# Float64 weights made float32: loaded two bytes further on, and put together from integer parts

## The chip, the cores and the metric

The kernel runs on one core of one Trainium2 chip, as a single launch. The metric is the device time of that launch in microseconds. Three runs of the kernel before gave 390.85, 390.97 and 391.49 us; the median is 390.97 us.

A core has five engines that run side by side, each through its own list of instructions, in order: TensorE (PE in the profile, with its weight loads as PEld), VectorE (DVE), ScalarE (ACT), GpSimd (POOL) and SyncE (SP), which here does nothing but issue transfers. Sixteen DMA engines carry the transfers.

## The reference, cut to what matters

A Mamba-2 scan over `x`, `a`, `B`, `C` (4 sequences, 8 heads, 768 steps) gives 3072 tokens of 256 numbers. They pass through a normalised SwiGLU network:

```
rms = np.sqrt(np.mean(x * x, axis=-1, keepdims=True) + 1e-06)
xn = x / rms * rms_g
g = xn @ w_gate                       # 256 x 1536
silu = g * (1.0 / (1.0 + np.exp(-g)))
val = xn @ w_val                      # 256 x 1536
return (silu * val @ w_out).astype(np.float32)   # 1536 x 256
```

The three weight matrices are drawn as float32 and then multiplied by a float64 scalar, so they arrive as float64: 8 bytes a number, 3 x 1536 x 256 of them. [...] A float64 is one sign bit, 11 bits of exponent and 52 of mantissa; seen as four 16-bit words in memory, word 3 (the last) holds the sign, the exponent and the first 4 bits of the mantissa, and words 0, 1 and 2 hold the rest from the bottom up.

## The kernel before, in words

All work is written as a flat list of small steps. Two dictionaries (`first_kinds`, `kinds`) name them, and a long string `order` gives their sequence by hand: `0:man.3` is the step `man` with argument 3 of block 0. Every engine gets its instructions in the sequence of that string; nothing is re-ordered later. Six blocks of 512 tokens follow one another; the scan of a block is done beside the network of the block before it. The network of blocks 1 to 5 uses fast matrix products of the Strassen kind (`product_gv`, L965, and `product_o`, L1086), on sums of weights that are made once (`combine_w`, L934). Block 0 uses plain products (L879, L889, L997) in its first part, while the weights still come in.

The weights come in 18 pieces of 512 numbers on each of 128 partitions (512 KB each): pieces 0 and 1 hold 128 columns of both gate and value matrix, pieces 2 to 11 hold 256 columns of one of the two, pieces 12 to 17 hold two row blocks of the output matrix. Each piece takes four named steps:

- `fetch.k` (L171) issues the transfers from SP into a buffer `wr`, of which there are six in turn. Pieces 0 and 1 take two transfers of 256 KB with rows of 1024 bytes, all others one of 512 KB with rows of 2048 bytes.
- `pow.k` (`power`, L217) makes the power of two and the sign, as bfloat16, with three ScalarE activations (all on line L215): word 3 to an int16, that to float32, that to the int16 whose bits are the bfloat16.
- `man.k` (`mantissa`, L231) makes the mantissa as a float32 between 2^20 and 2^21 in magnitude, with two VectorE instructions: L234 (masks of the high 32-bit word, with the leading one set) and L237 (adds the low word times 2^-32).
- `wt.k` (`weight`, L240) multiplies the two into `wgv` or `wo`, with one VectorE instruction, L243.

A buffer `wr` is free for the next piece after the first ScalarE step, L234 and L237 have read it. The tile `e` of the power shares its four buffers with the copies `p` that the fast products need (L971).

Pieces 0 to 9 and 11 are converted before the steps of the fast products begin in `order` (with `P.2.3`); piece 10 and the six pieces of the output matrix are converted between those products.

Of the kernel before, what the change touches and what calls it, by code (L numbers as in the profile page):

```python
# [9 lines left out]
FP32 = mybir.dt.float32  # L10
I32 = mybir.dt.int32
I16 = mybir.dt.int16
U32 = mybir.dt.uint32
BF16 = mybir.dt.bfloat16
AF = mybir.ActivationFunctionType
ALU = mybir.AluOpType
# [4 lines left out]
def kernel(  # L21
# [33 lines left out]
    nc = tc.nc  # L55

    P = 128
# [5 lines left out]
    DM, DF = moe_w_gate.shape  # L63
# [10 lines left out]
    const = ctx.enter_context(tc.tile_pool(name="const", bufs=1))  # L74
    raw = ctx.enter_context(tc.tile_pool(name="raw", bufs=3))
    ssd = ctx.enter_context(tc.tile_pool(name="ssd", bufs=2))
    cvt = ctx.enter_context(tc.tile_pool(name="cvt", bufs=2))
# [77 lines left out]
    wo = const.tile([P, NF, DM], FP32, name="wo")  # L155

    def words(w):
        t = w.tensor
        return dataclasses.replace(
            t, dtype=I32, shape=tuple(t.shape[:-1]) + (2 * t.shape[-1],)).ap()  # L160

    wsrc = {"g": words(moe_w_gate).rearrange("(t p) f -> p t f", p=P),
            "v": words(moe_w_val).rearrange("(t p) f -> p t f", p=P),
            "o": words(moe_w_out).rearrange("(o i) m -> i o m", i=P)}
    wdst = {"g": wg, "v": wv, "o": wo}
    pieces = [("gv", 0, P), ("gv", P, P)]
    pieces += [(n, c, 256) for c in range(256, DF, 256) for n in "gv"]
    pieces += [("o", c, 2) for c in range(0, NF, 2)]
    fetched = {}

    def fetch(*ks):  # L171
        for k in ks:
            n, c, w = pieces[k]
            if n == "o":
                src, dst, shape = wsrc[n][:, c:c + w], wo[:, c:c + w], (w, DM)
            else:
                src, shape = [wsrc[m][:, :, 2 * c:2 * (c + w)] for m in n], (2 * len(n), w)
                dst = (wgv.rearrange("p n k f -> p (n k) f") if n == "gv" else
                       wdst[n])[:, :, c:c + w]
            r = raw.tile([P, shape[0], 2 * shape[1]], I32, tag="wr", name="wr", bufs=6)  # L180
            if n == "o":
                nc.sync.dma_start(out=r, in_=src)
            else:
                for m, of in enumerate(src):
                    nc.sync.dma_start(out=r[:, 2 * m:2 * m + 2], in_=of)
            w32 = r.rearrange("p k (f w) -> p k f w", w=2)
            w16 = r.bitcast(I16).rearrange("p k (f w) -> p k f w", w=4)
            fetched[k] = (w16[:, :, :, 3], (w32[:, :, :, 0], w32[:, :, :, 1]), dst,
                          [P] + list(shape))

    parts = {}
# [3 lines left out]
    def functions(name):  # L202

        if loaded[0] != name:
            loaded[0] = name
            if name == "silu":
                nc.scalar.preload_act_table(AF.Silu)
            else:
                nc.scalar.preload_act_table_set("natural_log_exp_and_others")

    def activation(**operands):
        kind = {AF.Silu: "silu", AF.Exp: "exp", AF.Ln: "exp"}.get(operands["func"])
        if kind:
            functions(kind)
        nc.scalar.activation(**operands)  # L215

    def power(k):  # L217
        words16, (lo, hi), dst, shape = fetched[k]
        n = shape[1] * shape[2]
        e = cvt.tile([P, n], FP32, tag="e", name="e", bufs=4)  # L220
        k16 = e.bitcast(I16)[:, n:2 * n].rearrange("p (a b) -> p a b", a=shape[1])
        g = e.rearrange("p (a b) -> p a b", a=shape[1])
        b16 = e.bitcast(I16)[:, 0:n].rearrange("p (a b) -> p a b", a=shape[1])
        activation(out=k16, in_=words16, func=AF.Relu, scale=1.0 / 16, bias=kinks[:, 0:1])
        activation(out=g, in_=k16, func=AF.Prelu, scale=-1.0, bias=kinks[:, 1:2],
                             alpha=2.0 ** -20)
        activation(out=b16, in_=g, func=AF.Prelu, scale=-2.0 ** 27, bias=kinks[:, 2:3],
                             alpha=2.0 ** -20)
        parts[k, "e"] = b16.bitcast(BF16)

    def mantissa(k):  # L231
        words16, (lo, hi), dst, shape = fetched[k]
        m = cvt.tile(shape, I32, tag="m", name="m")
        nc.vector.tensor_scalar(out=m, in0=hi, scalar1=0xFFFFF, scalar2=0x100000,  # L234
                                op0=ALU.bitwise_and, op1=ALU.bitwise_or)
        parts[k, "f"] = f = m.bitcast(FP32)
        nc.vector.scalar_tensor_tensor(out=f, in0=lo.bitcast(U32), scalar=2.0 ** -32, in1=m,  # L237
                                       op0=ALU.mult, op1=ALU.add)

    def weight(k):  # L240
        words16, (lo, hi), dst, shape = fetched[k]
        e, f = parts.pop((k, "e")), parts.pop((k, "f"))
        nc.vector.scalar_tensor_tensor(out=dst, in0=f, scalar=2.0 ** -20, in1=e,  # L243
                                       op0=ALU.mult, op1=ALU.mult)

    a_sb = ffn.tile([NAR, 2 * P], FP32, tag="ob", name="a_sb", bufs=1)
    warm = const.tile([P, 256], BF16, name="warm")
# [15 lines left out]
    ident16 = const.tile([P, P], BF16, name="ident16")  # L263
    whole16 = const.tile([P, P], BF16, name="whole16")
    never16 = const.tile([P, HC], BF16, name="never16")
    kinks = const.tile([P, 3], FP32, name="kinks")
    mean = const.tile([P, P], FP32, name="mean")
    eps = const.tile([P, 1], FP32, name="eps")
    tmask = const.tile([P, 2], FP32, name="tmask")
# [63 lines left out]
            nc.vector.tensor_copy(out=never16[r], in_=never[r, r])  # L333

    def kinks_of_powers():
        for k, v in enumerate((1152.0 - 7.5 / 16, 256.0, -1792.0 * 128.0)):
            nc.vector.memset(kinks[:, k:k + 1], v)

    def idle(n):
# [23 lines left out]
    def minus_mid():  # L363
# [17 lines left out]
                                               op0=ALU.mult),  # L381
        "mid": from_middle, "middles": from_middles,
        "never16": mask16, "ident16": lambda: nc.vector.tensor_copy(out=ident16, in_=ident),
        "whole16": lambda: nc.vector.tensor_copy(out=whole16, in_=never),
        "kinks": kinks_of_powers, "eps": lambda: nc.vector.memset(eps, 1e-6),
        "mean": lambda: nc.vector.memset(mean, 1.0 / DM),
        "tmask": lambda: nc.vector.reduce_sum(
            out=tmask, in_=hmask.rearrange("p (q t) -> p t q", t=2), axis=AX.X),
# [9 lines left out]
    rows, ps = {}, {}  # L398
# [797 lines left out]
    def by_vector(out, in_, scale):  # L1196
# [22 lines left out]
        "yt": lambda p: taken_out(p, ac.copy),  # L1219
        "ydone": lambda p: leave(("y", p)),  # L1220
        "pow": power, "man": mantissa, "wt": weight,
        "ms": norm_sums, "rs": norm_roots, "rb": spread_roots, "xn": norm_apply,
        "early": lambda f, s: products_early(
# [15 lines left out]
        "cw": combine_w, "cwp": lambda j, k: combine_w(j, k, nc.gpsimd), "o": first_projection,  # L1239
        "tx": combine_x, "txp": lambda blk, k: combine_x(blk, k, nc.gpsimd),  # L1240
        "fetch": fetch, "put": put,
    }

# [249 lines left out]
```

## Time and profile before

| | |
|---|---|
| median of three runs | 390.97 us (390.85 to 391.49) |
| span of the profiled execution, first to last instruction | 389.5 us |
| PE busy | 383.3 us (98%) |
| DVE busy | 289.8 us (74%) |
| ACT busy | 226.4 us (58%) |
| POOL busy | 152.0 us (39%) |
| granted TensorE clock | 1.000 |
| DMA packets, bytes | 109940, 28.05 MB |

The profile shows one execution. Its span runs from the first to the last instruction; 390.97 - 389.5 = 1.5 us of the median run lie around it, and the page gives no other time for the profiled execution. "Busy" is the union of the times of an engine's instructions. For PE it is a weak sign, since matmuls overlap and their ends are modelled: an idle time of PE is real, but a busy one can hide waiting, which shows as a group of matmuls that takes longer than the same group elsewhere. A transfer's "landing" is the time from its issue until its semaphore tells that the data is there.

### The profile page before, as it was taken

How to read it: one execution, taken by the hardware profiler on the slowest of the kernel's cores; microseconds unless marked ns; L12 is line 12 of the kernel's file. 1: busy time of each engine (PE TensorE's matmuls, PEld its weight loads, DVE VectorE, ACT ScalarE, POOL GpSimd, SP SyncE). 2: the span in 40 equal slices, each digit the busy share in tenths (PEclk: the TensorE clock that was granted, in tenths of full speed). 3: DMA queues.
4: the chain of work that ended last, by engine and by line, in shares of the span. 5: the costliest groups of instructions: out<-in, count | busy, mean ns of one | idle time of the engine just before them, and what ended most of it. 6: DMA issues, size and time to landing. Idle time of an engine off the chain costs nothing.

```text
span 389.5 us, 9637 instructions
## 1 busy us (share of the span) xinstructions
PE 383.3 (98%) x3805; PEld 329.8 (85%) x3805; DVE 289.8 (74%) x612; ACT 226.4 (58%) x471; POOL 152.0 (39%) x168
## 2 busy tenths in 40 slices
PE   8999999999999999999999999999999999999996
PEld 5676478788888999888899988899888899988995
DVE  6999999997976988669594765768374577454684
ACT  2899979988767262665865234763444571345420
POOL 5022045523693455343577701364611234212231
PEclk9999999999999999999999999999999999999999
DMA  8978984474073414634336112000100001000001
GB/s 107 241 153 259 240 195 147 120 157 42 3 101 86 50 13 94 145 42 96 70 78 81 27 42 42 2 15 22 56 3 2 2 12 50 29 0 0 2 0 56
DMA packets 109940, 28.05 MB, mean 72 GB/s; under 512 B 94824, under 2 KB 103752, under 8 KB 109896
## 3 DMA queue, kind: packets, MB, share of 16 engines
q1 hardware_dynamic: 107816, 27.31, 32.8%
q8 instruction: 30, 0.49, 0.5%
q10 hardware_dynamic: 2080, 0.13, 0.4%
q14 instruction: 14, 0.11, 0.1%
HBM read 23.69 MB, written 3.74 MB: 70 GB/s over the span
## 4 chain that ended last, share of the span: by engine, by line
PE 87%; DVE 9%; issue 2%; ACT 1%; DVEq 0%; ACTq 0%
PE gate L965 29%; PE o L1086 23%; PE val L965 21%; PE o L997 5%; PE y L750 3%; PE g L613 1%; DVE wgv L243 1%; DVE m L237 1%; DVE m L234 1%; DVE hid L912 1%; PE g L606 1%; PE e L474 1%; PE y L678 1%; DVE L L652 1%; ACT yt L821 0%
## 5 line engine op out<-in xcount | busy, mean ns | idle before, releaser
L977 DVE TENSOR_TENSOR c<-val,p 128x512 f32<-128x512 f32 x99 | 67.4, 686 | 45.1 <-PE val L965 33.3
L971 ACT COPY p<-gate 128x512 f32<-128x512 f32 x99 | 56.8, 581 | 57.5 <-PE gate L965 55.4
L965 PE MATMUL gate<-tx,wgv 128*128 128x256 f32 x264 | 65.9, 381 | 0.0
L215 ACT ACTIVATE c<-c 128x256 f32<-128x256 f32 x99 | 40.0, 415 | 38.7 <-DVE c L977 38.4
L990 POOL TENSOR_TENSOR hid<-c 128x256 f32<-128x256 f32 x31 | 24.7, 800 | 87.1 <-ACT c L215 83.1
L965 PEld LDWEIGHTS gate<-tx,wgv 128*128 128x128 f32 x264 | 49.2, 190 | 7.3 <-ACT p L971 0.7
L1117 DVE TENSOR_TENSOR ob<-ob,o 128x128 f32<-128x128 f32 (+1 forms) x90 | 24.2, 298 | 21.7 <-PE o L1086 16.9
L990 DVE TENSOR_TENSOR hid<-c 128x256 f32<-128x256 f32 x68 | 34.5, 521 | 6.9 <-ACT c L215 6.7
L1086 PE MATMUL o<-two,hid 128*128 128x128 f32 x280 | 36.5, 276 | 0.1
L1086 PEld LDWEIGHTS o<-two,hid 128*128 128x128 f32 x280 | 34.5, 192 | 1.1 <-DVE hid L990 0.4
L965 PE MATMUL val<-xn,wgv 128*128 128x256 f32 x132 | 33.7, 381 | 0.0
L965 PE MATMUL val<-tx,sw 128*128 128x256 f32 x132 | 33.5, 380 | 0.0
L965 PE MATMUL val<-xn,sw 128*128 128x256 f32 x132 | 33.3, 381 | 0.0
L965 PE MATMUL gate<-tx,sw 128*128 128x256 f32 x132 | 33.1, 381 | 0.0
L965 PE MATMUL gate<-xn,wgv 128*128 128x256 f32 x132 | 32.8, 381 | 0.0
L507 POOL TENSOR_SCALAR_AFFINE_SELECT L<-L 64x512 f32<-64x512 f32 x32 | 23.6, 737 | 18.6 <-ACT L L215 17.4
L965 PEld LDWEIGHTS val<-xn,wgv 128*128 128x128 f32 x132 | 24.8, 190 | 3.5
L965 PEld LDWEIGHTS val<-tx,sw 128*128 128x128 f32 x132 | 24.8, 190 | 3.5 <-issue 0.2
L965 PEld LDWEIGHTS gate<-tx,sw 128*128 128x128 f32 x132 | 24.7, 190 | 3.5 <-ACT p L971 0.2
L965 PEld LDWEIGHTS gate<-xn,wgv 128*128 128x128 f32 x132 | 24.3, 190 | 3.4 <-DVE hid L912 0.3
L965 PEld LDWEIGHTS val<-xn,sw 128*128 128x128 f32 x132 | 24.4, 190 | 3.2 <-issue 0.2
L215 ACT ACTIVATE e<-e,kinks 128x512 f32<-128x512 int16 (+1 forms) x36 | 26.0, 722 | 1.2
(203 smaller groups left out, 717.0 us busy)
## 6 DMA issues: line engine op xcount, KB each, us to landing
L<-rowd SPq DMA_DIRECT2D x32, 128.0 KB, 3.4
xr<-in_x_dram SPq DMA_DIRECT2D x24, 128.0 KB, 3.2
wr<-in_moe_w_out_dram SPq DMA_DIRECT2D x6, 512.0 KB, 5.6
out_dram<-ob SPq DMA_DIRECT2D x24, 128.0 KB, 1.8
wr<-in_moe_w_gate_dram SPq DMA_DIRECT2D x5, 512.0 KB, 5.8
wr<-in_moe_w_val_dram SPq DMA_DIRECT2D x5, 512.0 KB
br<-in_B_dram SPq DMA_DIRECT2D x23, 64.0 KB, 2.6
dT<-rowe SPq DMA_DIRECT2D x10, 128.0 KB
```

What stands on the lines that cost most here:

```text
L215: nc.scalar.activation(**operands)
L234: nc.vector.tensor_scalar(out=m, in0=hi, scalar1=0xFFFFF, scalar2=0x100000, op0=ALU.bitwise_and, op1=ALU.bitwise_or)
L237: nc.vector.scalar_tensor_tensor(out=f, in0=lo.bitcast(U32), scalar=2.0 ** -32, in1=m, op0=ALU.mult, op1=ALU.add)
L507: nc.gpsimd.affine_select(out=L[r], in_=L[r], pattern=[[0, L.shape[1]], [1, HC]], compare_op=ALU.is_ge, fill=0.0, base=0, channel_multipli ...
L750: nc.tensor.matmul(out=y[2 * k + u][rows, (2 * n + i) * HC:(2 * n + i + 1) * HC], start=(k, u, rows.start) not in opened, stop=True, skip_ ...
L965: nc.tensor.matmul(out=dst[:, half[w]], lhsT=lhsT, rhs=rhs, start=(k in (1, 2, 5) and w == 0), stop=True, skip_group_check=True)
L971: nc.scalar.copy(out=t, in_=Xs[j])
L977: nc.vector.tensor_tensor(out=t, in0=Zs[j], in1=a, op=ALU.add)
L990: engine.tensor_tensor(out=hid[:, 2 * j + c // 10 - 1, c % 10 - 1], in0=u, in1=src[:, half[1]], op=ALU.mult)
L997: nc.tensor.matmul(out=o, lhsT=hid[:, f, k // 2, (k % 2) * P:(k % 2 + 1) * P], rhs=wo[:, f], start=opens, stop=(f == NF - 1), skip_group_c ...
L1086: nc.tensor.matmul(out=Os[blk, b][:, place * P:(place + 1) * P], lhsT=hidden_or_sum(u)[:, g], rhs=rhs, start=(blk, b) not in opened, stop= ...
L1117: nc.vector.tensor_tensor(out=o, in0=o, in1=src, op=ALU.add if what[0] == "+" else ALU.subtract)
```

## The change

Each row is fetched without its first two bytes. The transfer starts at the second 16-bit word of a row and takes one word less (2046 bytes of 2048, or 1022 of 1024), and lands at the start of the buffer's row. In the buffer every number's words are thereby shifted by one place: word 3 is found at place 2, and words 1 and 2, which were on either side of a 32-bit boundary, now are one aligned 32-bit word at place 0. Word 0, the lowest 16 bits, is not used any more.

- `power` has two ScalarE steps in place of three. The first turns word 3 into a float32, the second into an int32 that equals (word 3 - 14336) times 2^19 with the sign in the top bit: the float32's sign, exponent and first 4 mantissa bits.
- `mantissa` has one VectorE step in place of two: the 32-bit word times 2^-13, at most 2^19 - 1, as an integer. Those are the other 19 bits of the mantissa.
- `weight` puts the two together with a bitwise or of two int32 tiles (`tensor_tensor`), in place of the product of two tiles and a constant (`scalar_tensor_tensor`).
- `kinks`, the constants of the ScalarE steps, has two columns in place of three.

The string `order`, the pieces, the buffers and their number stay as they are. The lists of instructions of PE, POOL and SP keep their sequence and number; DVE's and ACT's lose the instructions named and keep the sequence of the others.

```diff
-            t, dtype=I32, shape=tuple(t.shape[:-1]) + (2 * t.shape[-1],)).ap()
+            t, dtype=I16, shape=tuple(t.shape[:-1]) + (4 * t.shape[-1],)).ap()
...
-                src, dst, shape = wsrc[n][:, c:c + w], wo[:, c:c + w], (w, DM)
+                src, dst, shape = [wsrc[n][:, c:c + w]], wo[:, c:c + w], (w, DM)
             else:
-                src, shape = [wsrc[m][:, :, 2 * c:2 * (c + w)] for m in n], (2 * len(n), w)
+                src, shape = [wsrc[m][:, :, 4 * c:4 * (c + w)] for m in n], (2 * len(n), w)
...
-            r = raw.tile([P, shape[0], 2 * shape[1]], I32, tag="wr", name="wr", bufs=6)
-            if n == "o":
-                nc.sync.dma_start(out=r, in_=src)
-            else:
-                for m, of in enumerate(src):
-                    nc.sync.dma_start(out=r[:, 2 * m:2 * m + 2], in_=of)
-            w32 = r.rearrange("p k (f w) -> p k f w", w=2)
-            w16 = r.bitcast(I16).rearrange("p k (f w) -> p k f w", w=4)
-            fetched[k] = (w16[:, :, :, 3], (w32[:, :, :, 0], w32[:, :, :, 1]), dst,
-                          [P] + list(shape))
+            r = raw.tile([P, shape[0], 4 * shape[1]], I16, tag="wr", name="wr", bufs=6)
+            for m, of in enumerate(src):
+                rows = of.shape[1]
+                nc.sync.dma_start(out=r[:, rows * m:rows * (m + 1), 0:4 * shape[1] - 1],
+                                  in_=of[:, :, 1:])
+            w16 = r.rearrange("p k (f w) -> p k f w", w=4)
+            w32 = r.bitcast(U32).rearrange("p k (f w) -> p k f w", w=2)
+            fetched[k] = w16[:, :, :, 2], w32[:, :, :, 0], dst, [P] + list(shape)
...
     def power(k):
-        words16, (lo, hi), dst, shape = fetched[k]
+        top, below, dst, shape = fetched[k]
         n = shape[1] * shape[2]
         e = cvt.tile([P, n], FP32, tag="e", name="e", bufs=4)
-        k16 = e.bitcast(I16)[:, n:2 * n].rearrange("p (a b) -> p a b", a=shape[1])
         g = e.rearrange("p (a b) -> p a b", a=shape[1])
-        b16 = e.bitcast(I16)[:, 0:n].rearrange("p (a b) -> p a b", a=shape[1])
-        activation(out=k16, in_=words16, func=AF.Relu, scale=1.0 / 16, bias=kinks[:, 0:1])
-        activation(out=g, in_=k16, func=AF.Prelu, scale=-1.0, bias=kinks[:, 1:2],
-                             alpha=2.0 ** -20)
-        activation(out=b16, in_=g, func=AF.Prelu, scale=-2.0 ** 27, bias=kinks[:, 2:3],
-                             alpha=2.0 ** -20)
-        parts[k, "e"] = b16.bitcast(BF16)
+        activation(out=g, in_=top, func=AF.Prelu, scale=-1.0, bias=kinks[:, 0:1],
+                   alpha=2.0 ** -40)
+        activation(out=g.bitcast(I32), in_=g, func=AF.Prelu, scale=-2.0 ** 59,
+                   bias=kinks[:, 1:2], alpha=2.0 ** -40)
+        parts[k, "e"] = g.bitcast(I32)
 
     def mantissa(k):
-        words16, (lo, hi), dst, shape = fetched[k]
-        m = cvt.tile(shape, I32, tag="m", name="m")
-        nc.vector.tensor_scalar(out=m, in0=hi, scalar1=0xFFFFF, scalar2=0x100000,
-                                op0=ALU.bitwise_and, op1=ALU.bitwise_or)
-        parts[k, "f"] = f = m.bitcast(FP32)
-        nc.vector.scalar_tensor_tensor(out=f, in0=lo.bitcast(U32), scalar=2.0 ** -32, in1=m,
-                                       op0=ALU.mult, op1=ALU.add)
+        top, below, dst, shape = fetched[k]
+        parts[k, "f"] = m = cvt.tile(shape, I32, tag="m", name="m")
+        nc.vector.tensor_scalar(out=m, in0=below, scalar1=2.0 ** -13, scalar2=2.0 ** 19 - 1,
+                                op0=ALU.mult, op1=ALU.min)
 
     def weight(k):
-        words16, (lo, hi), dst, shape = fetched[k]
+        top, below, dst, shape = fetched[k]
         e, f = parts.pop((k, "e")), parts.pop((k, "f"))
-        nc.vector.scalar_tensor_tensor(out=dst, in0=f, scalar=2.0 ** -20, in1=e,
-                                       op0=ALU.mult, op1=ALU.mult)
+        nc.vector.tensor_tensor(out=dst.bitcast(I32), in0=f, in1=e, op=ALU.bitwise_or)
...
-        for k, v in enumerate((1152.0 - 7.5 / 16, 256.0, -1792.0 * 128.0)):
+        for k, v in enumerate((-14336.0, -28672.0 * 2.0 ** 19)):
```

More of the change, by code (lines that the diff above doesn't have):

```diff
@@ L265 @@
     never16 = const.tile([P, HC], BF16, name="never16")
-    kinks = const.tile([P, 3], FP32, name="kinks")
+    kinks = const.tile([P, 2], FP32, name="kinks")
     mean = const.tile([P, P], FP32, name="mean")
```

## The prediction

> **What bounds the kernel now.** I began with the page's busy shares and its chain of waits (with the first and the last of the chain's pieces on DVE in this part: start, duration), then looked at the stretches in which weights are converted, and then at PE's own waits there.
>
> ```profile
> PE 383.3 (98%) x3805; PEld 329.8 (85%) x3805; DVE 289.8 (74%) x612; ACT 226.4 (58%) x471; POOL 152.0 (39%) x168
> PE 87%; DVE 9%; issue 2%; ACT 1%; DVEq 0%; ACTq 0%
> ...
> 16.18 0.06 DVE L L652
> ...
> 53.49 0.21 DVE A L692
> ```
>
> PE is idle for 389.5 - 383.3 = 6.2 us of the whole span, and the chain that ends last is PE for 87% of it. The 9% of DVE in that chain, about 35 us, lie together, from 16.2 to 53.7 us. The view by stretches shows that part (columns: PE, PEld, DVE, ACT, POOL busy with counts, clock, DMA share, GB/s):
>
> ```profile
> 10.00:20.00 10.00, 9.35 (x172) 6.38 (x172) 9.35 (x20) 8.70 (x16) 0.00 (x0) 1.00 0.92 225
> 20.00:30.00 10.00, 9.93 (x150) 7.59 (x139) 9.59 (x23) 9.77 (x18) 2.18 (x2) 1.00 0.82 171
> 30.00:40.00 10.00, 9.96 (x61) 5.77 (x60) 9.86 (x18) 9.81 (x17) 2.25 (x3) 1.00 0.90 267
> 40.00:50.00 10.00, 10.00 (x141) 4.67 (x142) 9.69 (x22) 8.81 (x14) 0.00 (x0) 1.00 0.90 228
> 50.00:60.00 10.00, 9.50 (x126) 7.73 (x108) 9.61 (x22) 8.25 (x20) 6.13 (x8) 1.00 0.83 185
> 60.00:110.00 50.00, 49.98 (x372) 42.86 (x371) 46.10 (x86) 42.12 (x76) 23.75 (x25) 1.00 0.40 89
> ```
>
> Four resources are nearly full at once from 10 to 60 us: PE, DVE, ACT and the DMA engines. A chain can follow only one of them, and it follows DVE. Whether DVE's time is worth anything must be read from what PE loses, as everything after 60 us is PE without a gap (49.98 of 50 us).
>
> PE's waits for another engine between 10 and 60 us are two, in the view of waits (total us, times, longest) and in PE's timeline (start, duration, releaser in brackets):
>
> ```profile
> PE y L719 <- DVE S L700: 0.5, 1, 0.5
> PE g L613 <- ACT sq L215: 0.5, 1, 0.5
> ...
> 33.04 3.60 PE L879 MATMUL gate<-xn,wgv 128*128 128x512 f32 x8
> 36.57 1.16 PE L613 MATMUL g<-T 32*64 32x128 f32 x32
> 37.65 7.13 PE L879 MATMUL gate<-xn,wgv 128*128 128x512 f32 x16
> ...
> 55.70 0.70 PE L613 MATMUL g<-T 32*64 32x128 f32 x32 [0.50 <-ACT sq L215]
> ```
>
> A third is hidden in busy time: the 32 products of L613 take 1.16 us at 36.57 and 0.70 us at 55.70, so 0.46 us of the first are waiting. The long products hide none: 8 of L879 start over 3.53 us (33.04 to 36.57) and 16 over 7.07 us, the same 0.44 us each. PE is thus the bound here too, and DVE and ACT only just keep up.
>
> **The change part by part.** The conversion's instructions, by their tiles (ns min/median/max):
>
> ```profile
> L234 DVE TENSOR_SCALAR m<-wr x18: 410/420/717, 15.0 to 92.5; 128x512 int32<-128x512 int32 x18
> L237 DVE SCALAR_TENSOR_TENSOR m<-wr,m x18: 691/693/1106, 15.4 to 93.0; 128x512 f32<-128x512 uint32 x18
> L215 ACT ACTIVATE e<-wr,kinks x18: 743/760/800, 17.0 to 86.2; 128x512 int16<-128x512 int16 x18
> L215 ACT ACTIVATE e<-e,kinks x36: 721/722/724, 17.9 to 87.8; 128x512 f32<-128x512 int16 x18, 128x512 int16<-128x512 f32 x18
> L243 DVE SCALAR_TENSOR_TENSOR wgv<-m,e x12: 681/687/1025, 20.0 to 62.1; 128x512 f32<-128x512 f32 x12
> ...
> 36.93 0.68 DVE L912 TENSOR_TENSOR hid<-u,hid 128x512 f32<-128x512 f32 x1
> ```
>
> *DVE.* L237 goes: 18 x 0.69 = 12.4 us less, 11 of the 18 (7.6 us) before 54 us. L234 stays one instruction over the same words at the same stride, now a multiply and a minimum on integers, which no row shows. Ends: 0.42 us as L234, or 0.69 us as L237, which reads such integers for arithmetic. I take 0.42, as the shape and kind of instruction are L234's; with 0.69 a piece still saves 0.42. L243 becomes a product of two tiles without a constant: L912 has 0.68 us for that shape, L243 0.69, so nothing changes. One memset of `kinks` less is nothing.
>
> *ACT.* One of the two 0.722 us steps goes: 18 x 0.72 = 13.0 us less. The first step writes float32 in place of int16 and the second int32: bounds 0.72 and 0.80 from the rows above, so nothing more than 0.08 us either way; I take none.
>
> *What that is worth on PE.* At 18.5 to 19.0 us PE waits for DVE's states. DVE's timeline before it, with two later rows and one of ACT:
>
> ```profile
> 14.98 0.42 DVE L234 TENSOR_SCALAR m<-wr 128x512 int32<-128x512 int32 x1
> 15.44 0.69 DVE L237 SCALAR_TENSOR_TENSOR m<-wr,m 128x512 f32<-128x512 uint32 x1
> 16.18 2.35 DVE L652 TENSOR_TENSOR L<-g,L 128x1024 f32<-128x1024 f32 x2
> ...
> 36.60 0.42 DVE L587 TENSOR_TENSOR T<-tp,dT 128x256 f32<-128x256 f32 x1
> 53.41 0.48 DVE L692 TENSOR_TENSOR A<-y,tmask 128x128 f32<-128x128 f32 x2
> ...
> 15.53 1.04 ACT L215 ACTIVATE L<-e 128x1024 f32<-128x1024 f32 x1
> ```
>
> Piece 0's L237 stands right before L652. Without it L652 can begin up to 0.69 us sooner, and its second half, from about 17.3 us, can too, as the exponentials it needs end at 16.57 on ACT. That covers the wait of 0.52. Next late there are the products g of L606 on PE, which also feed L652; if these hold it, less is won. At 36.57 the products g wait for banks whose last reader is DVE (L587 at 36.60); five pieces' L237 have then gone, 3.5 us, so 0.46 goes. At 55.2 they wait for ACT's squares, which stand behind DVE's L692 (53.41) and piece 11's ScalarE steps: 11 pieces sooner on both, so 0.50 goes. The next to bind is PE's own sequence, in which all three places are followed at once by long products that have their operands.
>
> Sum: 0.52 + 0.46 + 0.50 = 1.48 us. The rest of the 20 us taken off DVE and ACT before 60 us, 11 x (0.69 + 0.72) = 15.5, becomes idle time. After 60 us there is nothing to win: PE idles 0.02 us to 110 us. Against the profiled execution this is 389.5 - 1.5 = 388.0 us of span; the median lies 1.5 us above the span, so 389.5 us.
>
> *Transfers.* SP issues the same transfers in the same sequence. The buffer `wr` comes free one DVE instruction sooner, which lets later fetches start sooner or changes nothing. What a row of 2046 bytes that starts two bytes off costs, no row shows: all transfers of before start at whole multiples of their row. Bounds: the same as now, or, if each row is handled twice (once as it is, once to shift or complete it), twice the time. I take the same, since bytes and number of rows are the same; the other end is the second rival. If the cover were gone, what would be late is this:
>
> ```profile
> wr<-in_moe_w_gate_dram SPq DMA_DIRECT2D x5, 512.0 KB, 5.8
> ...
> 33.63 0.76 SPq L185 DMA_DIRECT2D wr<-in_moe_w_gate_dram  x1
> ...
> 41.95 0.37 SPq L185 DMA_DIRECT2D wr<-in_moe_w_gate_dram  x1
> ...
> 38.99 0.76 ACT L215 ACTIVATE e<-wr,kinks 128x512 int16<-128x512 int16 x1
> ...
> 59.75 0.78 ACT L215 ACTIVATE e<-wr,kinks 128x512 int16<-128x512 int16 x1
> ```
>
> The pairs are pieces 8 and 10. Piece 8 is the tightest: 5.4 us (33.63 to 38.99) from issue to first use, about what such a transfer takes to land (5.8 us median), so with less than 2 us to spare. ACT does not idle before it. Piece 10 has 17.8 us.
>
> [...]
>
> **The rivals.**
>
> *1. Only idle time is made.* PE is full, and the three waits could be replaced at once by others (the banks by the products before them, ACT's squares by the state products). For it: PE's idle time in all of 20 to 50 us is 0.11 us. Against it: each of the three has its releaser on an engine that gets 0.7 to 7.6 us of room. It gives 390.9 us, within 0.2% (0.8 us, about what a measurement of this kernel can tell from no change).
>
> *2. Slower: the transfers become the bound.* Rows that begin and end off their boundaries could cost twice the time. The DMA engines are busy 0.92, 0.82, 0.90, 0.90 and 0.83 of the five stretches to 60 us: 43.7 of 50 us, so 6.3 us are free. At 267 GB/s for a share of 0.90, a full rate of 297 GB/s, a piece of 0.524 MB takes 1.77 us, and the 14 pieces after the first that are issued by 60 us take 24.7 us. The free time is gone when a piece costs 6.3 / 24.7 = 25% more. That is the point from which it decides. At twice the price the excess is 24.7 - 6.3 = 18.4 us by 60 us; four of these pieces (10, and 12, 13 and 15, which are used after it) are not needed until 59.75 us, which takes 4 x 1.77 = 7.1 us off. PE then starts its unbroken part about 11 us later: about 401 us. The same queue carries x, B and the rows of the decays, so these would be late as well. For it: the engines' shares. Against it: no byte more is moved, and the rows stay long.
>
> [...]
>
> *3. The chain at its word.* If the 7.6 us of L237 before 54 us were all on the path, as the chain's view has it, the time would be 390.97 - 7.6 = 383.4 us. Against it: PE would have to be idle or stretched by as much, and only 1.5 us are found.
>
> **How the numbers follow.** The forecast, 0.60: between 388.9 (the 0.6 us beyond 1.48 that small stretches of PE may hold) and 390.2 (half of 1.48), likeliest 389.5. Rival 1: 0.16, 390.2 to 391.7, a little of it beyond 0.2% slower, when shifted instructions meet in a worse way. Rival 2: 0.19, from 392 at a price 30% up to 401 at double. Rival 3: 0.05. Faster by more than 0.2% (under 390.19): the forecast nearly whole and rival 3, 0.63. Same: 0.14. Slower: rival 2 and the tail of rival 1, 0.23. The range 388.3 to 395 leaves out rival 3 and the dearer half of rival 2, about 0.15. The likeliest case's own range is 388.9 to 390.2.
>
> **What would show it.** Right: L237 is gone and DVE's busy time is about 277 us, ACT's 213; the first step on `wr` takes DVE 0.42 us; PE's waits on S, on the banks at 36 us and on the squares are gone; DVE and ACT show idle time between 20 and 60 us; the chain is PE nearly throughout from 17 us on; the fetches land in 4 to 6 us as before. Wrong: transfers of `wr` that land later, waits of ACT or DVE on a DMA, and a DMA share near 1 to 60 us (rival 2); PE's waits in the same places with other releasers (rival 1); DVE's first step at 0.69 us, which takes back part of the gain.

## The result and the profile after

The changed kernel takes 389.42 us (median of 4 runs, 388.91 to 389.88) against 391.0 us for the kernel before (4 runs, 390.85 to 391.49). The ratio is 0.9952 with a 95% interval of 0.9938 to 0.9967, so about 1.9 us are gained, between 1.3 and 2.4. The profiled execution has a span of 388.0 us, 1.5 us less than before. The forecast was 389.5 us and 388.0 us of span. The total came out; of the three waits that made it up, one did not move, and one went in some executions only.

From the page of the kernel after: busy times, the chain of waits by engine, the packets, the queue that carries the fetches.

```profile
PE 382.5 (99%) x3805; PEld 330.0 (85%) x3805; DVE 277.8 (72%) x593; ACT 214.3 (55%) x453; POOL 150.1 (39%) x168
...
DMA packets 109940, 28.04 MB, mean 72 GB/s; under 512 B 94824, under 2 KB 107848, under 8 KB 109896
...
q1 hardware_dynamic: 107816, 27.30, 33.9%
...
PE 97%; DVE 1%; ACT 1%; issue 0%; ACTq 0%; DVEq 0%
```

DVE lost 12.0 us and ACT 12.1 us, and the chain left DVE: PE has 97% of it where it had 87%. The queue carries as many packets as before, so no row was split; the rows of 2046 bytes now count as "under 2 KB". Its share of time is 33.9% where it was 32.8% before; e4 and e5 below bear on how much of that is due to the rows.

The stretches, with the columns of before (PE, PEld, DVE, ACT, POOL busy with counts, clock, DMA share, GB/s):

```profile
10.00:20.00 10.00, 9.35 (x168) 6.38 (x168) 8.65 (x19) 7.97 (x15) 0.00 (x0) 1.00 0.92 236
20.00:30.00 10.00, 10.00 (x151) 7.62 (x144) 9.44 (x22) 7.90 (x15) 2.44 (x3) 1.00 0.84 146
30.00:40.00 10.00, 10.00 (x61) 5.80 (x60) 6.78 (x15) 7.77 (x13) 1.95 (x3) 1.00 0.84 238
40.00:50.00 10.00, 10.00 (x171) 4.77 (x169) 8.44 (x21) 7.78 (x13) 1.12 (x1) 1.00 0.99 270
50.00:60.00 10.00, 10.00 (x91) 8.40 (x75) 8.60 (x20) 7.58 (x18) 5.55 (x7) 1.00 0.89 190
```

DVE and ACT now have 0.6 to 3.2 us of idle time in each 10 us, and PE lost its gaps, but for 0.65 us in the first stretch, which is as large as it was.

The conversion's instructions by tile, and the landing of `wr` (ns min/median/max, first and last start), then the landing in the kernel before:

```profile
L224 DVE TENSOR_SCALAR m<-wr x18: 411/420/814, 15.0 to 91.1; 128x512 int32<-128x512 uint32 x18
L230 DVE TENSOR_TENSOR wgv<-m,e x12: 680/684/1021, 20.1 to 60.2; 128x512 int32<-128x512 int32 x12
L208 ACT ACTIVATE e<-wr,kinks x18: 742/763/800, 17.1 to 84.8; 128x512 f32<-128x512 int16 x18
L208 ACT ACTIVATE e<-e,kinks x18: 721/722/725, 17.9 to 85.6; 128x512 int32<-128x512 f32 x18
DMA to landing us min/median/max: 4.2/5.5/6.6
```

```profile
DMA to landing us min/median/max: 4.2/4.9/7.4
```

Every duration is that of the instruction whose place it took: 0.42, 0.68, 0.76 and 0.72 us. The range of the landing, 4.2 to 6.6 us, lies inside that of before (4.2 to 7.4). The median is 0.6 us longer, but that is not the mark of a shifted row: it is 5.1 us in e1, the same kernel again, and 5.4 us in e5, which fetches whole rows.

The three places at which PE was to win, in PE's timeline, with the VectorE instructions that the first two hang on and SP's issue of the transfer that the second of these needs:

```profile
19.07 0.77 PE L705 MATMUL y<-T,S 32*64 32x128 f32 x16 [0.52 <-DVE S L686]
36.48 1.11 PE L599 MATMUL g<-T 32*64 32x128 f32 x32
54.60 0.69 PE L599 MATMUL g<-T 32*64 32x128 f32 x32
...
33.19 0.60 SPq L566 DMA_DIRECT2D dT<-rowe  x1
...
16.23 2.35 DVE L638 TENSOR_TENSOR L<-g,L 128x1024 f32<-128x1024 f32 x2 [0.78 <-PE g L592]
36.46 0.42 DVE L573 TENSOR_TENSOR T<-tp,dT 128x256 f32<-128x256 f32 x1 [1.32 <-DMA dT<-rowe]
```

The wait on S is still 0.52 us: VectorE reaches L638 0.78 us early and then waits for PE's products g. At 36.48 the 32 products still take 1.11 us: VectorE is idle for 1.32 us until `dT`, a row of decays that goes out to memory and comes back, has landed. Only at 54.60 is the wait gone.

So where do 1.48 us come from? PE runs the same 3805 products in the same sequence in both kernels, so the k-th of one profile can be set against the k-th of the other. How much earlier it starts after the change, read at the steps (worked out from the two traces):

```
time before   earlier by   what changed there
up to 27      0.00 us
28.2          0.09         row sums L488
49.1          0.32         y L750
51.8          0.52         gate L965
55.7          1.09         products g L613
74.0          1.10
75.1          1.39         gate L965
289.6         1.48         gate L965
```

Two of these steps can be seen in single rows of the kernel before and of the kernel after (VectorE's states ahead of y; the weight loads of PE's gate product):

```profile
47.16 0.69 DVE L237 SCALAR_TENSOR_TENSOR m<-wr,m 128x512 f32<-128x512 uint32 x1
48.10 0.92 DVE L702 SCALAR_TENSOR_TENSOR S<-S,fcol,A 128x64 f32<-128x64 f32 x3
48.71 0.73 PE L750 MATMUL y<-T,S 32*64 32x64 f32 x32
74.75 0.73 PEld L965 LDWEIGHTS gate<-tx,wgv 128*128 128x128 f32 x4 [0.42 <-ACT p L971]
```

```profile
48.57 0.49 PE L736 MATMUL y<-T,S 32*64 32x64 f32 x32
73.25 0.84 PEld L951 LDWEIGHTS gate<-tx,wgv 128*128 128x128 f32 x4
```

The 32 products y took 0.73 us because their states ended at 49.02 behind a piece's L237; now they take 0.49. At 74.75 PE's weight load waited 0.42 us for ACT's copy `p`, which stood behind two steps of 0.72 us; now it waits for nothing. The step at 51.8 is of the same kind: before, PE's weight load waited 0.27 us there for VectorE's `hid`. None of the three was in the list of waits as an idle time of PE.

### The profile page after: what moved, and what is told of

Same layout as the page of the kernel before. It is cut to its first block, busy times and chain, and to the rows that moved or that the text cites. A ratio compares the mean times of both kernels' runs of the same rounds, so it can differ in the third digit from the quotient of the medians.

```text
span 388.0 us, 9604 instructions
## 1 busy us (share of the span) xinstructions
PE 382.5 (99%) x3805; PEld 330.0 (85%) x3805; DVE 277.8 (72%) x593; ACT 214.3 (55%) x453; POOL 150.1 (39%) x168
## 3 DMA queue, kind: packets, MB, share of 16 engines
q1 hardware_dynamic: 107816, 27.30, 33.9%
## 4 chain that ended last, share of the span: by engine, by line
PE 97%; DVE 1%; ACT 1%; issue 0%; ACTq 0%; DVEq 0%
PE gate L951 29%; PE o L1072 23%; PE val L951 22%; PE o L983 5%; PE gate L865 4%; PE y L736 3%; PE gate L875 2%; PE g L599 2%; PE e L460 1%; PE g L592 1%; PE y L664 1%; PE tp L540 1%; PE e L474 0%; DVE ob L1103 0%; PE idle L328 0%
## 5 line engine op out<-in xcount | busy, mean ns | idle before, releaser
L976 POOL TENSOR_TENSOR hid<-c 128x256 f32<-128x256 f32 x31 | 23.8, 769 | 89.6 <-ACT c L208 84.9
L1072 PE MATMUL o<-two,hid 128*128 128x128 f32 x280 | 36.5, 276 | 0.1
L951 PE MATMUL val<-xn,wgv 128*128 128x256 f32 x132 | 33.7, 381 | 0.0
L951 PE MATMUL val<-tx,sw 128*128 128x256 f32 x132 | 33.5, 380 | 0.0
L493 POOL TENSOR_SCALAR_AFFINE_SELECT L<-L 64x512 f32<-64x512 f32 x32 | 22.8, 713 | 18.1 <-ACT L L208 16.8
L208 ACT ACTIVATE u<-gate 128x256 f32<-128x256 f32 (+1 forms) x37 | 14.6, 402 | 18.2 <-PE gate L951 15.3
```

The costliest lines, as they stand in the source:

```text
L493: nc.gpsimd.affine_select(out=L[r], in_=L[r], pattern=[[0, L.shape[1]], [1, HC]], compare_op=ALU.is_ge, fill=0.0, base=0, channel_multipli ...
L951: nc.tensor.matmul(out=dst[:, half[w]], lhsT=lhsT, rhs=rhs, start=(k in (1, 2, 5) and w == 0), stop=True, skip_group_check=True)
L976: engine.tensor_tensor(out=hid[:, 2 * j + c // 10 - 1, c % 10 - 1], in0=u, in1=src[:, half[1]], op=ALU.mult)
L1072: nc.tensor.matmul(out=Os[blk, b][:, place * P:(place + 1) * P], lhsT=hidden_or_sum(u)[:, g], rhs=rhs, start=(blk, b) not in opened, stop= ...
```

## The experiments

The kernels ran in three groups (e1 to e4, e5 to e8, e9 to e11), each on one chip beside the kernel before, and ratios are to that kernel in the same group. In e2 and e3 a step is put back on one engine, in e4 on both.

**e1_after_again**: the changed kernel once more, nothing edited.

> The changed kernel once more, for its time beside the others on the same chip and for a second profile. Its four runs so far lie in two pairs about 0.9 us apart (388.91 and 389.08; 389.76 and 389.88), and the profile is of the slower pair. Theory A (the early transfers fall a little differently from run to run, and the converted pieces wait for them by turns): a profile of the faster pair shows fewer waits on a DMA between 30 and 45 us. Theory B (the pairs have nothing to do with the conversion): the two profiles agree up to 110 us within 0.2 us. Both: 389.4 us, 389.0 to 389.9.

Measured: 389.19 us, ratio 0.9952 [0.9938, 0.9966]; span 387.5 us. In this execution the second place is won (SP's queue, VectorE, PE):

```profile
31.79 0.60 SPq L566 DMA_DIRECT2D dT<-rowe  x1
35.46 0.42 DVE L573 TENSOR_TENSOR T<-tp,dT 128x256 f32<-128x256 f32 x1 [0.67 <-DMA dT<-rowe]
36.49 0.69 PE L599 MATMUL g<-T 32*64 32x128 f32 x32
```

In the first profile after, SP issued this transfer at 33.19. Set product against product, the two executions differ by 0.45 us here and nowhere else by as much. The place at 36.5 us is won or not by when a transfer lands, in one and the same kernel.

**e2_dve_back**: a third VectorE step of 0.69 us per piece is put back; ScalarE and the transfers stay changed.

```diff
+        nc.vector.scalar_tensor_tensor(out=m, in0=below, scalar=0.0, in1=m,
+                                       op0=ALU.mult, op1=ALU.add)
```

> The changed kernel with a third VectorE step put back in every piece, of the kind that went (the 32-bit word times 0 plus the mantissa, into the mantissa, so that the value stays). ScalarE keeps its two steps. Theory A (what was won is PE's waits on VectorE, the ones at 48.7 us on the states and at 55 us on squares that stand behind VectorE's work): VectorE is full again from 20 to 54 us, the waits come back, 390.5 to 391.0 us. Theory B (ScalarE's third step was what mattered): within 0.3 us of the changed kernel, 389.4 to 389.7 us.

Measured: 390.69 us, ratio 0.9999 [0.9985, 1.0012]. The gain is gone, and so is VectorE's idle time; PE waits for the squares as before, and for S, as it does in the kernel after too (stretch, then waits):

```profile
30.00:40.00 10.00, 9.89 (x60) 5.68 (x59) 9.86 (x18) 7.44 (x12) 2.25 (x3) 1.00 0.88 253
```

```profile
PE y L707 <- DVE S L688: 0.5, 1, 0.5
PE g L601 <- ACT sq L208: 0.5, 1, 0.5
```

The squares are ACT's, and ACT has its relief here (7.44 of 10 us). The wait is back all the same: VectorE's queue sets when ACT can begin them. In ACT's timeline of e2 the copies `yt` just ahead of the squares wait 0.50 us, at 53.56 us, for VectorE's `A`.

**e3_act_back**: a third ScalarE step per piece is put back; VectorE stays changed.

```diff
+        nc.scalar.copy(out=g, in_=g)
```

> The changed kernel with a third ScalarE step put back in every piece (a copy of the float32 exponent onto itself), VectorE keeps its two steps. Theory A (VectorE mattered): 389.4 to 389.8 us, PE's wait on the squares at 55 us stays away or is under 0.2 us. Theory B (ScalarE mattered): 390.5 to 391.0 us.

Measured: 389.16 us, ratio 0.995 [0.9937, 0.9963], the time of the changed kernel, with ACT full again (the fourth column of busy times) and no wait on the squares:

```profile
30.00:40.00 10.00, 10.00 (x60) 5.46 (x59) 7.38 (x16) 9.78 (x15) 1.23 (x2) 1.00 0.95 266
```

Product against product it gives back 0.29 us against e1 behind the first 8 us: 0.19 at 73 us and 0.10 later. At the first of these PE's weight load waits for the copy `p` once more:

```profile
72.26 0.73 PEld L952 LDWEIGHTS gate<-tx,wgv 128*128 128x128 f32 x4 [0.33 <-ACT p L958]
```

The medians are too coarse for that. The copy takes 0.62 us, a little less than the step of 0.72 us that the change removed. The gain is VectorE's step but for some 0.3 us.

**e4_both_back**: both steps back; what stays changed is the transfers and the operations.

```diff
+        nc.scalar.copy(out=g, in_=g)
...
+        nc.vector.scalar_tensor_tensor(out=m, in0=below, scalar=0.0, in1=m,
+                                       op0=ALU.mult, op1=ALU.add)
```

> The changed kernel with both third steps put back: only the shifted rows are left of the change, as far as time goes. If rows of 2046 bytes that start two bytes off cost nothing, this is the time of the kernel before, 390.7 to 391.3 us. If they cost something that the room on VectorE and ScalarE hides in the changed kernel, it is slower than the kernel before, 391.5 us or more.

Measured: 391.25 us, ratio 1.0011 [0.9999, 1.0022]. With the work of VectorE and ScalarE close to what it was before, fetching the rows two bytes further on costs 0.4 us by the ratio and 0.9 us at the most by its interval, which also holds no cost at all. The queue's share is 33.0% here, against 32.8% for the whole rows of the kernel before.

**e5_aligned**: the changed kernel with whole rows, which begin at their boundary, and the words read where they lie in them.

```diff
-                nc.sync.dma_start(out=r[:, rows * m:rows * (m + 1), 0:4 * shape[1] - 1],
-                                  in_=of[:, :, 1:])
+                nc.sync.dma_start(out=r[:, rows * m:rows * (m + 1)], in_=of)
...
-            fetched[k] = w16[:, :, :, 2], w32[:, :, :, 0], dst, [P] + list(shape)
+            fetched[k] = w16[:, :, :, 3], w32[:, :, :, 0], dst, [P] + list(shape)
```

> The changed kernel with whole rows of 2048 (1024) bytes fetched from their start into the start of the buffer's rows; the same instructions then read word 3 for the exponent and words 0 and 1 for the mantissa's lower 19 bits, so those bits of the weights are wrong here; nothing else is left out. Theory A (a shifted and shortened row costs what a whole one does): 389.2 us as the changed kernel beside it, within 0.3, and the median landing of a piece within 0.5 us of the changed kernel's. Theory B (the shift has a price that the room on the engines hides, as PE is the bound): pieces land sooner, ACT's and DVE's waits on a DMA between 30 and 45 us go, and 388.7 us or less.

Measured: 389.13 us, ratio 0.9949 [0.9934, 0.9963]. The queue's time (its share of 16 engines' span, last column) against the 33.9% of the shifted rows:

```profile
q1 hardware_dynamic: 107816, 27.31, 33.5%
```

The second profile of the shifted kernel has 33.7%. Whole rows are not faster in the time, and the queue's share differs by 0.2 to 0.4 points. How finely this is known: e1 and e5 ran in different groups, their ratios differ by 0.0003, and each has an interval of some 0.0015 (0.6 us) to either side.

**e6_quarter_more** and **e7_double** ask how near the second rival was: behind each fetch of a piece, a quarter of it, or all of it, is moved once more, into a spare place in memory that nothing reads. The diff is of e6; e7 has 4 for 1.

```diff
+                j = dram.tile([P, rows, shape[1] * 1], I16, name="junk%d_%d" % (k, m))
+                nc.sync.dma_start(out=j[:, :, 0:shape[1] * 1 - 1],
+                                  in_=of[:, :, 1:shape[1] * 1])
```

> The changed kernel with a second transfer behind each fetch, of a quarter of its columns (rows of 512 or 256 bytes less two) into DRAM, that nobody reads: a quarter more to carry for the weights, and one issue more on SP each. By the prediction's arithmetic (6.3 us free of 50 against 24.7 us of pieces) this is the point from which transfers decide: 389.3 to 390.5 us, with DMA shares of 0.95 or more to 60 us. A rival reading (the engines' shares count time that is not needed, and each piece has more room than that): no change, 389.2 us within 0.3. A second rival (the tightest pieces decide, not the sum, and they already wait): 391 us or more.

> The changed kernel with each fetch followed by a second of the same size into DRAM that nobody reads: the weights' transfers at twice the price. The prediction's second rival, at its worst: PE starts its unbroken part about 11 us later, 400 us (398 to 403). If the sum over the engines is not what counts but each piece's own room (2 to 9 us), less: 392 to 396 us. If the transfers have far more room than I think: under 390.5 us.

Measured: 394.98 us, ratio 1.0095 [1.0074, 1.0115], and 406.92 us, ratio 1.042 [1.0395, 1.0445]: 5.8 and 17.8 us above e5 of the same group. Waits of e6 between 10 and 60 us, then its first and fourth stretch:

```profile
DVE T L576 <- DMA dT<-rowe: 3.9, 2, 2.8
PE A_ps L667 <- DMA xr<-in_x_dram: 2.6, 1, 2.6
```

```profile
10.00:20.00 10.00, 7.38 (x110) 4.99 (x111) 6.63 (x11) 6.51 (x13) 0.00 (x0) 0.89 0.77 194
...
40.00:50.00 10.00, 9.54 (x56) 4.15 (x60) 7.96 (x17) 5.61 (x9) 0.00 (x0) 0.83 0.90 251
```

A quarter more costs 5.8 us, though the DMA engines are not full (0.77 and 0.90). What PE hangs on is not a piece but what stands in the queue with the pieces: an x that it needs in the first 20 us, and the row `dT`. The edit adds more than bytes, however. Each extra transfer must also be issued by SP, and in e6 its rows are short (510 and 254 bytes). SP's queue in the kernel after, then in e6:

```profile
10.28 1.35 SPq L150 DMA_DIRECT2D xr<-in_x_dram  x2
```

```profile
8.62 0.65 SPq L187 DMA_DIRECT2D junk<-in_moe_w_gate_dram  x1
...
13.08 1.51 SPq L150 DMA_DIRECT2D xr<-in_x_dram  x2
```

Four extra issues of 0.55 to 0.65 us each stand ahead of this x. It is issued 2.8 us later than in the kernel after, and PE's wait for it is 2.6 us. A row that only took longer to move would need no extra issue. So e6 and e7 do not measure the price of a dearer row, and no run here separates the load of the DMA engines from the time of SP.

Part of the price is not a wait: the granted clock falls to 0.89 in the first stretch and to 0.83 in the fourth. Product against product with e1, PE loses about 1.4 and 1.8 us in these two places while it runs at the lower clock. In e7 the clock falls further (stretch, then PE's timeline around it):

```profile
40.00:50.00 10.00, 5.17 (x38) 2.48 (x37) 7.04 (x15) 3.63 (x6) 0.00 (x0) 0.67 0.94 295
```

```profile
36.88 3.60 PE L868 MATMUL gate<-xn,wgv 128*128 128x512 f32 x8
43.06 0.47 PE L602 MATMUL g<-T 32*64 32x128 f32 x12 [2.58 <-DVE hid L889]
45.77 1.12 PE L602 MATMUL g<-T 32*64 32x128 f32 x20 [2.25 <-DVE T L576]
46.82 5.42 PE L868 MATMUL gate<-xn,wgv 128*128 128x512 f32 x8
```

Eight products of L868 take 3.60 us ahead of the two waits of 2.6 and 2.3 us and 5.42 us behind them: 1.8 us that no view of waits lists.

**e8_fetch7_later**: can the place at 36.5 us be won in every execution? Fetch 7, which is issued just ahead of the row transfers, is moved behind them.

```diff
-        0:g.1.1/0 0:L.1.1 0:Tl.1 0:g.1.0/2 0:exp.1.0 0:L.1.0 0:fetch.4 0:last.0 0:Tl.0 0:fetch.7
+        0:g.1.1/0 0:L.1.1 0:Tl.1 0:g.1.0/2 0:exp.1.0 0:L.1.0 0:fetch.4 0:last.0 0:Tl.0
...
-        0:scale.3 0:eps 0:early.0.0/0 0:early.0.1 0:rowout.0 0:ms.0 0:parts.1 0:pow.3 0:pow.2 0:wt.3
+        0:scale.3 0:eps 0:early.0.0/0 0:early.0.1 0:rowout.0 0:fetch.7 0:ms.0 0:parts.1 0:pow.3 0:pow.2 0:wt.3
```

> The changed kernel with the step that fetches piece 7 moved behind the two stores of the row decays and row sums in SP's queue (from in front of the spread of pair 2's decays to behind the second row store), so that those stores, which the next spread waits for, no longer stand behind its 512 KB. Theory A (at 36.5 us PE's products g now wait for a VectorE step that waits for the spread of pair 3's decays): that spread lands one to two us sooner, VectorE's waits on it (3.1 us in the changed kernel's first profile, 0.9 in its second) go, and so does PE's wait of up to 0.4 us: 388.9 us, 0.3 faster than the changed kernel beside it, and less spread between runs. Theory B (the products g take 1.1 us there by themselves): no change, 389.2 us.

Measured: 390.09 us, ratio 0.9981 [0.9964, 0.9998], 1.0 us slower than e5 of its group. Fetches 7 and 5 now follow each other, piece 5 lands later, and its VectorE step stands ahead of the one that PE waits for:

```profile
36.58 0.43 DVE L224 TENSOR_SCALAR m<-wr 128x512 int32<-128x512 uint32 x1 [1.89 <-DMA wr<-in_moe_w_val_dram]
37.69 0.65 PE L599 MATMUL g<-T 32*64 32x128 f32 x20 [1.50 <-DVE T L573]
```

That PE hangs on VectorE's step T there is confirmed; the edit made it later.

**e9_S0_first**: the mask product L.1.0 behind the state S.0 on VectorE, for the wait of 0.52 us.

```diff
-        0:g.1.1/0 0:L.1.1 0:Tl.1 0:g.1.0/2 0:exp.1.0 0:L.1.0 0:fetch.4 0:last.0 0:Tl.0 0:fetch.7
-        0:dT.2 0:tok 0:tokout 0:A.1 0:A.0 0:S.0 0:S.1 0:pow.0 0:wt.0 0:y.0/1 0:sq.0 0:pow.1 0:y.1/2
+        0:g.1.1/0 0:L.1.1 0:Tl.1 0:g.1.0/2 0:exp.1.0 0:fetch.4 0:last.0 0:Tl.0 0:fetch.7
+        0:dT.2 0:tok 0:tokout 0:A.1 0:A.0 0:S.0 0:L.1.0 0:S.1 0:pow.0 0:wt.0 0:y.0/1 0:sq.0 0:pow.1 0:y.1/2
```

> The changed kernel with one VectorE step moved: the mask product L.1.0 (L638) behind S.0 (L686, L688) instead of ahead of it. Nothing else is changed. It asks why the wait of 0.52 us of PE for S at 19.07 stayed when VectorE had been relieved. Theory (VectorE's order holds it: S stands behind two mask products of 1.2 us that wait for the products g, and the two behind each other are the hold): S is done about 1.2 us sooner, the wait of 0.52 us at 19.07 goes, and the kernel is 0.3 to 0.5 us faster than the changed one, about 388.8 us; the wait for L behind it must be none. Rival (PE is bound to wait there for something of that pair anyway): the wait moves to the next products y, which need L.1.0, now done 0.8 us later; the time stays within 0.2 us of 389.2 us.

Measured: 389.74 us, ratio 0.9967 [0.9954, 0.998], 0.6 us slower than the changed kernel by the ratios (0.9967 against 0.9952, with intervals that overlap). The first products y start at once, and the second wait for the mask product; product against product with e1, from 8 us on, PE has lost 0.4 us behind them (VectorE, PE):

```profile
17.45 1.22 DVE L638 TENSOR_TENSOR L<-g,L 128x1024 f32<-128x1024 f32 x1
17.43 0.45 PE L705 MATMUL y<-T,S 32*64 32x128 f32 x8
18.72 0.45 PE L705 MATMUL y<-T,S 32*64 32x128 f32 x8 [0.85 <-DVE L L638]
```

The rival holds, and harder than it was put: from the products g on, PE needs both mask products and the states from VectorE, some 3 us of work that cannot start before those products, and the sequence written is not the worse one. With the wait of 0.78 us for g ahead of it, this is why VectorE's relief is worth nothing at 19 us.

**e10_swap57**: fetch 5 in fetch 7's place, and fetch 7 right behind the transfer `dT.3`. **e11_both**: e9 and e10 together.

```diff
-        0:g.1.1/0 0:L.1.1 0:Tl.1 0:g.1.0/2 0:exp.1.0 0:L.1.0 0:fetch.4 0:last.0 0:Tl.0 0:fetch.7
+        0:g.1.1/0 0:L.1.1 0:Tl.1 0:g.1.0/2 0:exp.1.0 0:L.1.0 0:fetch.4 0:last.0 0:Tl.0 0:fetch.5
...
-        0:xn.0 0:turn.3 0:norm.0 0:T.3 0:Tt.3.1 0:Tt.2.1 0:fetch.5 0:Tt.3.0 0:exp.2 0:Td.2
-        0:early.1.0/1 0:early.1.1 0:dT.3 0:man.4 0:table.1 0:x.2 0:norm.1 0:man.5 0:Td.3 0:silu.0
+        0:xn.0 0:turn.3 0:norm.0 0:T.3 0:Tt.3.1 0:Tt.2.1 0:Tt.3.0 0:exp.2 0:Td.2
+        0:early.1.0/1 0:early.1.1 0:dT.3 0:fetch.7 0:man.4 0:table.1 0:x.2 0:norm.1 0:man.5 0:Td.3 0:silu.0
```

> The changed kernel with two fetches moved: piece 5 takes the place of piece 7 (behind Tl.0), and piece 7 is issued right behind the transfer dT.3. So no fetch of a piece shares the engines with the row transfers dT.2 and dT.3 between 28 and 33 us but one. It asks whether PE's wait for the bank at 36.5 us hangs on when dT.3 lands. Theory (dT.3 lands earlier when no piece is issued just ahead of it): VectorE's wait for dT on the second step shrinks from 1.32 us to under 0.7, the 32 products there take 0.7 us in place of 1.11, and the time is that of the executions which had it already, 388.7 to 389.0 us. Rival (the row's own two transfers, out to memory and back, decide): the wait for dT stays, and the time stays at 389.2 us; if piece 7 lands late, VectorE waits for it instead and the kernel is up to 0.9 us slower, as with the last edit.

> Both edits together, the step S.0 ahead of L.1.0 and the two fetches exchanged. If both theories hold, the gains add, 388.3 to 388.7 us, with no wait of PE over 0.1 us between 10 and 60 us; if only one holds, the time is that one's; if neither, 389.2 us.

Measured: e10 388.68 us, ratio 0.9946 [0.993, 0.9961]; e11 389.67 us, ratio 0.9967 [0.9953, 0.9982]. e10 has the lowest median of all, but its interval and the changed kernel's overlap almost wholly: it is faster than the kernel before and not shown to be faster than the kernel after. In its profile the 32 products take 0.74 us, as wanted, while VectorE still waits for the row:

```profile
35.03 0.42 DVE L573 TENSOR_TENSOR T<-tp,dT 128x256 f32<-128x256 f32 x1 [1.21 <-DMA dT<-rowe]
35.42 0.74 PE L599 MATMUL g<-T 32*64 32x128 f32 x32
```

Neither side of its expectation holds whole: the products are on time, and the row's own way out and back still takes VectorE 1.21 us of waiting. They are on time in e1 as well, without the edit, so one profile does not show that the edit did it. e11 adds nothing to e9.

## Why the prediction was right or wrong

*PE is the bound in 10 to 60 us, though the chain followed DVE there.* Right. With 12 us off each of the two engines, 1.5 us of span are gained; the third rival, which took the chain at its word, is out by 6 us. The same row in the chain that went from 87% to 97% shows what the chain's 9% of DVE were worth.

*The cost of each instruction.* Right: the integer multiply and minimum at 0.42 us (the bound of 0.69 is not reached), the bitwise or at 0.68, ScalarE's steps at 0.76 and 0.72. DVE's 277.8 and ACT's 214.3 us were forecast as 277 and 213.

*0.52 us for the wait on S.* This step failed. Its caveat was the mechanism: "Next late there are the products g of L606 on PE, which also feed L652; if these hold it, less is won". They hold it by 0.78 us, more than the 0.69 that was freed, so nothing is won. What was not looked up for the sum is when the products g end: VectorE took up L652 at 16.18 us before and takes it up at 16.23 now.

*0.46 us for the banks at 36.57.* Right in size (0.45 us in e1), wrong in what is next late: not "PE's own sequence" but a transfer, `dT`, whose landing differs between executions; the first profile won 0.05 us. The releaser of the step T was read on VectorE alone, and its other operand was not asked for. (Six pieces' L237 start ahead of L587 in the kernel before, not five; nothing hangs on that.)

*0.50 us for ACT's squares.* Right: 0.57. Of the two queues that were named for it, e2 and e3 show that it was VectorE's.

*"After 60 us there is nothing to win."* Wrong by 0.38 us, and between 27 and 52 us another 0.47 us came that were not in the sum (0.52 us in the table, less the 0.05 us of the banks). These are the "small stretches of PE" for which the forecast had kept up to 0.6 us; they came to 0.9 in the first profile, and in that execution stood in for the waits that stayed. That the total was right to 0.1 us is therefore luck in part: of the terms 0.52, 0.46 and 0.50 the profile had 0, 0.05 and 0.57. In e1, where the banks' wait went as well, the same comparison with the kernel before gives 1.97 us, more than the sum.

*What ScalarE's step is worth.* The sum let both engines share the credit. The step of ScalarE is worth about 0.3 us, all of it behind 60 us and most of it at one place.

*The first rival, only idle time is made.* It holds at one of the three places and in some executions at a second, but not for the whole. *The second, slower by the transfers.* Its price did not arise: shifted rows cost no time that e4 and e5 can see, where e4 leaves room for 0.9 us. The queue's share is the same within 0.4 points (33.9 and 33.7% against 33.5% with whole rows), at 107816 packets each. That each row might be handled twice, from which the rival took its double price, was an assumption of the author's; no trace shows how a single row is carried. The rival's point, 25% more with no loss there, was worked out from the free time of the DMA engines. It is not confirmed: with a quarter more moved e6 loses 5.8 us, and e7 loses 17.8 us at double where about 11 were worked out. Part of both is the time that SP takes to issue the extra transfers, so what a dearer row would cost stays open. What they do show is that an average of free time over 50 us says little of a queue in which a single x or row must be there at its moment, and that the lower clock behind PE's idle time comes on top (1.8 us in e7).

## What to carry to other kernels

When four engines are nearly full at once, relief of one is worth what the bound engine loses in waits, place by place (here 12 us off each of two engines gave 1.5 us of span); for each such place list every operand of the instruction waited for, the transfers too, and take the second latest as what remains. Waits also hide in a busy bound engine: compare groups of equal products (0.73 against 0.49 us) and the idle time of its weight loads, not its idle time alone. The free share of the transfer engines is not the room of a transfer queue (e6 loses 5.8 us at shares of 0.77 and 0.90): ask for its tightest transfer when it is issued, what stands ahead of it, and when it must have landed. And an experiment that adds transfers also adds issues (0.55 to 0.65 us each in front of e6's late x).

## What the runs showed of the hardware

The first 8 us of a program differ between executions of kernels that are the same there. PE's timeline of e1 and of e10:

```profile
6.52 1.19 PE L430 MATMUL full_ps<-la,early_ones 128*128 128x192 f32 x4
```

```profile
5.82 0.82 PE L430 MATMUL full_ps<-la,early_ones 128*128 128x192 f32 x4
```

The four products take 1.19 us in e1 and 0.82 us in e10, and by 7.5 us e10 is 1.07 us ahead (the next products, of L432, start at 7.54 in e1 and at 6.47 in e10), with no difference in the kernels up to there. The spans of two single profiles can thus differ by as much: e10's 387.1 us against e1's 387.5 is such a case, as e10 loses 0.67 us of its lead later. Only the comparison from 8 us on tells them apart. The clock column shows 1.00 there in both executions, but this need not be a reading: it shows 1.00 in the first profile of the kernel after as well, and there the trace has no clock record ahead of 7.28 us, where the first one, of full clock, starts. The four products start there at 6.51, 6.83, 7.15 and 7.38 us and the next one at 7.54: 0.32 us apart up to that moment, 0.23 across it and 0.16 behind it. In the kernel before, the first record, again of full clock, starts at 7.16 us, and these products start at 6.50, 6.83, 7.14, 7.32 and 7.48. So in both traces the pace doubles where the record of full clock starts. In e10 it changed earlier: two products of L460 take 0.65 us from 3.93 us on, where e1 takes 1.06. That moves everything behind it. How much of the spread between the runs of one kernel comes from it is not known, as only one run of each was profiled.

In e6 and e7 the granted clock falls behind PE's waits (0.83 and 0.67 in the fourth stretch). In e7, in and behind the fourth stretch (columns as above):

```profile
43.00:44.00 1.00, 0.47 (x12) 0.25 (x12) 0.33 (x1) 0.97 (x2) 0.00 (x0) 0.74 0.84 215
44.00:45.00 1.00, 0.00 (x0) 0.00 (x0) 0.00 (x0) 0.36 (x1) 0.00 (x0) 0.50 1.20 190
...
46.00:47.00 1.00, 1.00 (x21) 0.67 (x14) 1.00 (x3) 0.59 (x1) 0.00 (x0) 0.50 0.99 313
...
49.00:50.00 1.00, 1.00 (x2) 0.36 (x2) 1.00 (x3) 0.97 (x3) 0.00 (x0) 0.50 0.94 352
50.00:51.00 1.00, 1.00 (x3) 0.38 (x2) 0.90 (x3) 0.97 (x2) 0.00 (x0) 0.84 1.04 389
```

It is at 0.50 from 44 us to past 50 us, for four microseconds after PE is full again at 46. Worked out from this column, with the rest at full clock, it lasts 6.8 us: 0.52 us of the row at 43, six whole rows, and 0.32 us of the row at 50. In e6, counted the same way, the 0.83 of the fourth stretch is 3.4 us at 0.50. So PE's two waits of 2.6 and 2.3 us in e7, the second for a step T (VectorE's two of them wait 7.0 us for `dT` between 10 and 60 us), cost more than their length: the eight products behind them take 5.42 us in place of 3.60. That is a price of late transfers which the second rival had left out.
